# A seven-product matmul pass whose PSUM tiles go from two banks to one

## The chip, the cores and the metric

One NeuronCore of a Trainium2 chip runs the whole program. The metric is device time in microseconds, the median of three runs. A profile is one more execution, recorded by the hardware profiler.

## The reference

Attention over 4 batches, 12 heads, 448 positions and head size 64, with RMS-normed queries and keys; its output, 1792 tokens by 768 features, goes through two MLPs with 2048 hidden features:

```python
x = attention(q, k, v, g_q, g_k)              # (4*448, 768)
h = np.maximum(x @ moe_w_in, 0.0)             # first MLP
x = (h * h) @ moe_w_out
h = x @ moe2_w_in                             # second MLP
g = np.maximum(h, 0.0) + alpha * np.minimum(h, 0.0)
return g @ moe2_w_out
```

All of it is fp32. A product is taken in three matmuls of rounded parts ("hi" and "lo"): hi·lo, hi·hi, lo·hi. The lo part is the rest, x minus hi, so each operand costs a copy (hi) and a subtraction (lo).

## The kernel before

Features lie on the 128 partitions and the 448 tokens of one batch in the free dimension. Attention and the first MLP run first; they end near 814 us. From there to the end the second MLP runs as **seven-product passes**: batches are taken in pairs (0, 1), then (2, 3), and a 2 by 2 block product (two feature halves, two batches) is formed with seven products instead of eight, from sums of weight blocks and sums of activation blocks, the *forms*.

`quad` (L950) is one group of seven products. An **up** group makes hidden features from the three k-chunks of xs and xt (63 matmuls); a **down** group takes the hidden forms of two or three up groups (42 or 63 matmuls). `run_passes` (L1144) gives the order, the same for both batch pairs: u0 u1 u2, d0 (three groups, e = 0, 1, 2), u3 u4, d1 (three), u5 u6 u7, d2 (three). Panel d0 uses the forms of u0 and u1, d1 those of u2 to u4, d2 those of u5 to u7. That is 2 x 1008 = 2016 matmuls.

A group has four accumulators, called b, a, c and a scratch one, t. In the kernel before they lie in two PSUM tiles of two banks each, [128, 2, 512]: a and c are the halves of one tile, b and t the halves of the other (L952 and L953). `BANK` says where a product accumulates: A11, S2, S3 and A22 in b, A12 in a, S1 and S4 in c. An up group runs A11, A12, S2, S1, S3, S4, A22; a down group A11, S1, S2, S4, S3, A12, A22.

What happens after a product is in `event`. For an up group (L1001): `keep` copies an accumulator to an SBUF buffer q (ScalarE), before the next product accumulates onto it; `plus` adds or subtracts (VectorE, L995); `prelu` needs relu(-x) in a scratch accumulator and relu(x) (ScalarE, L1012 to L1018) and joins them (VectorE, L1020); `split` writes the hi copy of a form (ScalarE, L254) and its lo rest (VectorE or GpSimd, L262). For p5 the scratch of `prelu` is t, for p1 it is a, for u2 it is c. Two of the splits, `split((a, 0), 3, 2)` and `split((b, 0), 5, 2)`, take both halves of a tile, 896 columns, in one copy and one subtraction. Down groups add accumulators into the sums in SBUF (L1080).

The order on each engine is written out ahead of time by a list planner (`Tasks`, L53). Each step has an urgency, a duration (`act`, `dve`, `pool2`, L191 to L208) and what it reads and writes; the planner always issues the step that can start first. It keeps the halves of a PSUM tile apart, (a, 0) and (a, 1); the waits in the program come from the tile framework, which sees the tiles. A tile goes back to its pool when its last step is planned, and an up or down group takes all its tiles before its first product. Every engine works off its own queue in order.

`x_pair` (L1110) prepares the activation forms of the second batch pair: per k-chunk four loads of y from DRAM on the SyncE queue, seven hi copies, seven lo rests and four subtractions, through buffers of the pool q, of which there are nine at that time. It is called in `run_passes` while the last three down groups (d2) of the first pair are planned; each call's loads may not be planned before one given product of those groups (`begun`).

PSUM pool m (four tiles of two banks) also serves the end of the first MLP, whose tasks are planned before `ts.run(1)` (L1158).

Of the kernel before, what the change touches and what calls it, by code (L numbers as in the profile page):

```python
# [194 lines left out]
def dve(n):  # L195
    return 0.07 + 0.00104 * n
# [22 lines left out]
def attention_relu2_mlp_prelu_mlp(ctx: ExitStack, tc: tile.TileContext, qkt, qk_tm, v, gb, alpha, ident, sel,  # L219
# [10 lines left out]
    def pooled(pool, name, n, shape, dtype):  # L230
        ts.pool(name, [pool.tile(shape, dtype, name=f"{name}{i}") for i in range(n)])
# [592 lines left out]
    def without():  # L824
        with ExitStack() as es:
            q1 = es.enter_context(tc.tile_pool(name="q1", bufs=1))
            pp = es.enter_context(tc.tile_pool(name="pp2", bufs=1, space=PSUM))
# [121 lines left out]

            def quad(n, order, form, chunks, group, key, event):  # L950

                a, b = Buf(pool="m"), Buf(pool="m")  # L952
                place = {"a": (a, 0), "c": (a, 1), "b": (b, 0)}  # L953
                opened = set()
                turn[0] += 7
                t0 = turn[0]
# [3 lines left out]
                made = None if key in kept7 else sums(n, group, t0 - 24)  # L960

                def psum(x):
                    return x[0].ap[:, x[1], :S]

                for j, name in enumerate(order):
                    x, f = place[BANK[name]], FORM[name]
                    ts.phase = 1 if ahead and j < 3 else 2
                    if key is None:
                        w = unit(name, n, made, t0 + j - 17, None, None)
                    elif made:  # L970
                        k = Buf(dram.tile([128, 2, n], F32, name=f"k7_{key}_{j}"))
                        w = unit(name, n, made, t0 + j - 17, k, None)
                        kept7.setdefault(("made", key), []).append(k)
                    else:
                        w = unit(name, n, None, t0 + j - 17, None, kept7[key][j])
                    ts.phase = 2
                    start = BANK[name] not in opened
                    opened.add(BANK[name])
                    src = [form(f, k) for k in chunks]

                    for kk, get in enumerate(src):
                        def emit(e, w=w, x=x, kk=kk, get=get, fresh=start and not kk, more=not start, end=kk == len(src) - 1):
                            for part, h in ((0, 1), (0, 0), (1, 0)):
# [13 lines left out]
            def up(stage, q):  # L997
                s = slot_b[q % 3]
                p1, u2, p5 = (Buf(pool="q") for _ in range(3))

                def event(name, a, b, soon, psum):  # L1001
                    def ap(x):
                        return (lambda: x.ap) if isinstance(x, Buf) else (lambda: psum(x))
# [20 lines left out]
                    def split(x, f, n=1):  # L1024
                        def to(h):
                            return s.ap[:, f:f + n, h, :] if n > 1 else s.ap[:, f, h, :]

                        inside = isinstance(x, Buf)
                        items = [x] if inside else [(x[0], c) for c in range(2)]
                        src = ap(x) if inside else (lambda: x[0].ap[:, :, :S])  # L1030
                        add(soon, {"A": act(n * S, not inside)}, lambda e: copy(e, to(0), src()), items,
                            [(s, (f + i, 0)) for i in range(n)])
                        add(soon, {"V": dve(n * S), **({"P": pool2(S)} if inside else {})}, lambda e: rest(e, to(1), src(), to(0)),
                            items + [(s, (f + i, 0)) for i in range(n)], [(s, (f + i, 1)) for i in range(n)], free=not inside)

                    def plus(x, i0, i1, op=ALU.add):
                        add(soon, {"V": dve(S)}, tensor(ap(x), ap(i0), ap(i1), op), [y for y in (i0, i1) if y is not x], [x],
                            free=not all(isinstance(y, Buf) for y in (i0, i1)))

                    if name == "A11":  # L1040
                        keep(p1, (b, 0))
                    elif name == "A12":
                        plus(p1, (a, 0), p1)
                        prelu(p1, (a, 0), q)
                        split(p1, 0)
                    elif name == "S2":
                        keep(u2, (b, 0))
                    elif name == "S1":
                        keep(p5, (a, 1))
                    elif name == "S3":  # L1050
                        plus(p5, (b, 0), p5)
                        prelu(p5, (b, 1), q + KF // 2)
                        split(p5, 2)
                    elif name == "S4":
                        plus(u2, (a, 1), u2)
                        prelu(u2, (a, 1), q)
                        plus((a, 1), u2, p1, ALU.subtract)
                        plus((a, 0), p5, (a, 1), ALU.subtract)
                        split((a, 0), 3, 2)
                        plus((b, 1), (a, 0), p1, ALU.subtract)  # L1060
                    else:
                        c21, x = Buf(pool="q"), (b, 0)
                        prelu(c21, x, q + KF // 2, x)
                        split(c21, 1)
                        plus((b, 0), c21, (a, 0), ALU.subtract)
                        split((b, 0), 5, 2)

                quad(UP, UP_ORDER, lambda f, k: x_form(f, k), range(KD // 2), up32[q], f"u{q}", event)

            def down(p, e, batches):  # L1070
                held = {}

                def event(name, a, b, soon, psum):
                    first = p == 0

                    def keep(k, t, d, x):
                        held[k] = total[t][d] if first else Buf(pool="q")
                        add(soon, {"A": act(S, True)}, lambda e: copy(e, held[k].ap, psum(x)), [x], [held[k]])

                    def plus(k, t, d, x):  # L1080
                        y, z = held.get(k), total[t][d]
                        if k == "c21" and first:
                            keep(k, t, d, x)
                        else:
                            y = y or z
                            add(soon, {"V": dve(S)}, tensor(lambda: y.ap, lambda: psum(x), lambda: y.ap, ALU.add), [x], [y], free=True)
# [1 line left out]
                                add(soon, {"V": dve(S), "P": pool2(S)}, tensor(lambda: z.ap, lambda: z.ap, lambda: y.ap, ALU.add),  # L1088
                                    [y], [z])
                        if p == len(PANELS) - 1:  # L1090
                            add(soon, {"S": load(512 * S)}, dma(lambda: out[batches[t], d], lambda: z.ap), [z], [])

                    if name == "A11":
                        keep("p1", 0, e, (b, 0))
                    elif name == "S1":
                        keep("p5", 1, e + 3, (a, 1))
                    elif name == "S2":
                        keep("u2", 1, e, (b, 0))
                    elif name == "S4":
                        plus("u2", 1, e, (a, 1))  # L1100
                    elif name == "S3":
                        plus("p5", 1, e + 3, (b, 0))
                    elif name == "A12":
                        plus("p1", 0, e, (a, 0))
                    else:
                        plus("c21", 0, e + 3, (b, 0))

                quad(128 * len(PANELS[p]), DN_ORDER, lambda f, k: h_form(f, k), PANELS[p], dn32[e][p], None, event)

# [34 lines left out]
            def run_passes():  # L1144
                turn[0] = 40000
                for stage, batches in enumerate(((0, 1), (2, 3))):
                    for step in ("u0", "u1", "u2", "d0", "u3", "u4", "d1", "u5", "u6", "u7", "d2"):
# [18 lines left out]
                for d in range(KD):  # L1166
                    total[t][d].ap = sums_out[:, t, d, :]

            def more(name, n, shape, dt):
                for i in range(n):  # L1170
                    ts.free[name].append((ts.ends["T"], 200 + i, qb.tile(shape, dt, name=f"{name}_{i}")))
# [73 lines left out]
```

## Time and profile before

| | us |
|---|---|
| median of 3 runs | 1332.03 |
| lowest and highest run | 1327.61, 1338.84 |
| the profiled execution, own time | 1334.32 |
| its span | 1332.5 |
| mean granted TensorE clock in it | 0.968 |

PE is TensorE's matmuls, PEld its weight loads, DVE VectorE, ACT ScalarE, POOL GpSimd, SPq the SyncE queue that issues DMAs. In brackets behind an instruction stands the time in which its engine sat idle before it, and what ended that. PEclk is the granted TensorE clock as a share of full speed. Names m, q, ws, forms, xs, xt are tiles with their numbers left out: m is the PSUM pool, q and ws are both buffers of the SBUF pool q.

### The profile page before, as it was taken

Reading aid. Unit: us, or ns where it says so; the run is one execution under the profiler, and the core shown is the slowest. Engines: PE = TensorE matmul, PEld = TensorE weight load, DVE = VectorE, ACT = ScalarE, POOL = GpSimd, SP = SyncE. Lnnn points to the kernel's source line nnn. Section 1 sums busy time; section 2 is a strip of 40 time slices with the busy share of each in tenths; the row PEclk is TensorE's granted clock in tenths of the full one; section 3 lists DMA queues with packets and bytes.
Section 4 is the critical chain, followed back from the end, with each engine's and each line's share of the span. In section 5 each row is a group of like instructions: output and inputs, shape, how many; then the busy total and the mean of one; then the engine's idle time right before and its main releaser. Section 6 shows DMA issues by size and latency. Waiting matters only on the chain. (4 is left out here: it accounts for less than half of the span.)

```text
span 1332.5 us, 17324 instructions
## 1 busy us (share of the span) xinstructions
PE 1200.9 (90%) x5502; PEld 1023.2 (77%) x5502; DVE 901.7 (68%) x1596; ACT 792.3 (59%) x1561; POOL 526.2 (39%) x492
## 2 busy tenths in 40 slices
PE   4996998978999999999999999898888888979878
PEld 2554777767888888899999998687776767769767
DVE  6789999999887877137776504676657856554363
ACT  5787888886899788425552124555357435453452
POOL 3344356453555244200000067545566442135245
PEclk7998999999999999999999999898999899999999
DMA  5145758896546433579999956424154353422622
GB/s 179 52 152 201 240 179 278 276 320 247 187 151 199 157 132 106 185 253 333 325 322 340 323 193 224 162 110 167 48 206 166 123 203 116 148 82 78 195 71 83
DMA packets 95803, 250.32 MB, mean 188 GB/s; under 512 B 11296, under 2 KB 30880, under 8 KB 95712
## 3 DMA queue, kind: packets, MB, share of 16 engines
q1 hardware_dynamic: 95712, 249.22, 55.2%
q8 instruction: 43, 0.70, 0.2%
q14 instruction: 48, 0.39, 0.1%
HBM read 178.32 MB, written 70.78 MB: 187 GB/s over the span
## 5 line engine op out<-in xcount | busy, mean ns | idle before, releaser
L984 PE MATMUL m<-forms,whl 128*128 128x448 f32 x1008 | 219.2, 378 | 23.5 <-DVE forms L262 15.5
L984 PEld LDWEIGHTS m<-forms,whl 128*128 128x128 f32 x1008 | 195.4, 195 | 46.3 <-DVE forms L262 17.0
L984 PE MATMUL m<-xt,whl 128*128 128x448 f32 x432 | 111.0, 399 | 39.2 <-DVE q L995 13.9
L350 PE MATMUL bank<-xs,whl 128*128 128x448 f32 x576 | 138.0, 372 | 1.5 <-DMA whl<-w 1.5
L984 PEld LDWEIGHTS m<-xt,whl 128*128 128x128 f32 x432 | 84.4, 204 | 62.0 <-DVE q L1020 17.5
L350 PE MATMUL bank<-hg,whl 128*128 128x448 f32 x576 | 129.0, 367 | 2.0 <-DMA whl<-w 1.6
L984 PE MATMUL m<-xs,whl 128*128 128x448 f32 x576 | 124.7, 369 | 6.4 <-DVE xs L262 4.4
L984 PEld LDWEIGHTS m<-xs,whl 128*128 128x128 f32 x576 | 109.0, 190 | 17.2 <-DVE xs L262 4.7
L282 ACT ACTIVATE ws<-raw 128x384 f32<-128x384 f32 (+1 forms) x112 | 67.2, 600 | 92.2 <-DMA raw<-in_w 80.0
L350 PEld LDWEIGHTS bank<-xs,whl 128*128 128x128 f32 x576 | 108.6, 191 | 12.8 <-DMA whl<-w 1.9
L350 PE MATMUL m<-xs,whl 128*128 128x448 f32 x576 | 117.5, 366 | 0.7 <-ACT q L254 0.7
L350 PEld LDWEIGHTS bank<-hg,whl 128*128 128x128 f32 x576 | 108.1, 189 | 11.8 <-DMA whl<-w 2.0
L350 PE MATMUL m<-hg,whl 128*128 128x448 f32 x576 | 116.9, 365 | 0.0
L687 DVE TENSOR_REDUCE mc<-bank 112x1 f32<-112x448 f32 x192 | 111.3, 615 | 7.9 <-PE bank L683 6.5
L262 POOL TENSOR_TENSOR whl<-raw,whl 128x384 fp32r<-128x384 f32 (+1 forms) x87 | 87.2, 1006 | 74.2 <-ACT whl L254 64.9
L350 PEld LDWEIGHTS m<-xs,whl 128*128 128x128 f32 x576 | 107.9, 188 | 10.4 <-ACT q L254 1.1
L350 PEld LDWEIGHTS m<-hg,whl 128*128 128x128 f32 x576 | 108.2, 188 | 8.5
L262 POOL TENSOR_TENSOR whl<-ws,whl 128x384 fp32r<-128x384 f32 (+2 forms) x57 | 77.6, 1369 | 89.9 <-ACT whl L254 65.9
L708 PE MATMUL bank<-mv,st 128*128 128x448 f32 (+2 forms) x352 | 100.1, 390 | 7.7 <-DVE rhl L262 2.7
L262 POOL TENSOR_TENSOR xs<-q,xs 128x448 fp32r<-128x448 f32 x13 | 15.2, 1184 | 227.3 <-DMA q<-y 225.2
L286 DVE TENSOR_SCALAR ws<-ws 128x384 f32<-128x384 f32 (+1 forms) x112 | 46.2, 416 | 80.3 <-ACT ws L282 79.9
L254 ACT ACTIVATE whl<-raw 128x384 fp32r<-128x384 f32 (+1 forms) x120 | 59.5, 498 | 63.0 <-PE m L984 53.8
(166 smaller groups left out, 2353.0 us busy)
## 6 DMA issues: line engine op xcount, KB each, us to landing
raw<-in_w SPq DMA_DIRECT2D x64, 384.0 KB
raw<-in_w SPq DMA_DIRECT2D x48, 512.0 KB
whl<-w SPq DMA_DIRECT2D x64, 384.0 KB
whl<-w SPq DMA_DIRECT2D x48, 512.0 KB
k_u<-whl SPq DMA_DIRECT2D x56, 384.0 KB
whl<-k_u SPq DMA_DIRECT2D x56, 384.0 KB
w<-whl SPq DMA_DIRECT2D x32, 384.0 KB
w<-whl SPq DMA_DIRECT2D x24, 512.0 KB
```

What stands on the lines that cost most here:

```text
L254: nc.scalar.activation(out=o, in_=i, func=ACTF.Copy)
L262: (nc.gpsimd if e == "P" else nc.vector).tensor_tensor(out=o, in0=x, in1=hi, op=ALU.subtract)
L282: lambda e: nc.scalar.activation(out=f.ap[:, :n], in_=half(1).bitcast(F32), func=ACTF.Abs), [raw], [f], "f")
L286: lambda e: nc.vector.tensor_scalar(out=f.ap[:, :n], in0=f.ap[:, :n], scalar1=TINY, scalar2=None, op0=ALU.max),
L350: nc.tensor.matmul(out=acc.ap[:, t, :S], lhsT=w.ap[:, part * n + 128 * kk:part * n + 128 * kk + 128], rhs=src(h, k0 + kk, t)[1](), start=( ...
L687: lambda e, t=t, pm=pm: nc.vector.reduce_max(out=mc.ap[:, t:t + 1], in_=pm.ap[:CP, :S], axis=AX.X),
L708: nc.tensor.matmul(out=pa.ap[:keys, :S], lhsT=s.ap[:rows, k, c:c + keys], rhs=m.ap[:rows, k, :], start=(k == 0), stop=(k == 1))
L984: nc.tensor.matmul(out=psum(x), lhsT=w.ap[:, part * n + 128 * kk:part * n + 128 * kk + 128], rhs=get(h)[1](), start=fresh and h == 1, stop ...
```

## The change

1. Pool m now ends with the first MLP (`es_a`). After `ts.run(1)` a new PSUM pool n of eight one-bank tiles is opened in its place, and each group takes four of them, one per accumulator.
2. Every form is split by itself. In S4, form 4 (c) is split before form 3 (a), and form 6 (t) as soon as it is there; form 5 (b) is left for the end.
3. `x_pair` is called after all three d2 groups are planned. The loads of its first chunk are tied to a product 6 chunk-steps later than before (the third product of the first group instead of the first), those of the second 3 later, those of the third 15 earlier (the last product of the second group instead of the fifth of the third). The urgencies come to the same numbers.

```diff
-            pooled(pp, "m", 4, [128, 2, 512], F32)
-            for name in ("wf", "wsum"):
+            for name in ("wf", "wsum", "n"):
                 ts.pool(name, [])
             es_a = es.enter_context(ExitStack())
+            pooled(es_a.enter_context(tc.tile_pool(name="pp2", bufs=1, space=PSUM)), "m", 4, [128, 2, 512], F32)
...
-                a, b = Buf(pool="m"), Buf(pool="m")
-                place = {"a": (a, 0), "c": (a, 1), "b": (b, 0)}
+                place = {c: Buf(pool="n") for c in "bact"}
...
-                    return x[0].ap[:, x[1], :S]
+                    return x.ap[:, :S]
...
-                                         [x] + ([(a, "slot"), (b, "slot")] if not j and not kk else []), "mlp"))
-                    event(name, a, b, soon, psum)
+                                         [x] + ([(y, "slot") for c, y in place.items() if c != BANK[name]] if not j and not kk else []), "mlp"))
+                    event(name, *place.values(), soon, psum)
...
+                    def split(x, f):
+                        inside = x not in banks
+                        add(soon, {"A": act(S, not inside)}, lambda e: copy(e, s.ap[:, f, 0, :], ap(x)()), [x], [(s, (f, 0))])
+                        add(soon, {"V": dve(S), **({"P": pool2(S)} if inside else {})},
+                            lambda e: rest(e, s.ap[:, f, 1, :], ap(x)(), s.ap[:, f, 0, :]), [x, (s, (f, 0))], [(s, (f, 1))],
+                            free=not inside)
...
                     elif name == "S4":
-                        plus(u2, (a, 1), u2)
-                        prelu(u2, (a, 1), q)
-                        plus((a, 1), u2, p1, ALU.subtract)
-                        plus((a, 0), p5, (a, 1), ALU.subtract)
-                        split((a, 0), 3, 2)
-                        plus((b, 1), (a, 0), p1, ALU.subtract)
+                        plus(u2, c, u2)
+                        prelu(u2, c, q)
+                        plus(c, u2, p1, ALU.subtract)
+                        plus(a, p5, c, ALU.subtract)
+                        split(c, 4)
+                        split(a, 3)
+                        plus(t, a, p1, ALU.subtract)
+                        split(t, 6)
                     else:
...
-                        plus((b, 0), c21, (a, 0), ALU.subtract)
-                        split((b, 0), 5, 2)
+                        plus(b, c21, a, ALU.subtract)
+                        split(b, 5)
...
                             down(i, e, batches)
-                            if not stage and step == "d2":
-                                x_pair((2, 3), e, turn[0] - 8, begun[-(21, 21, 9)[e]])
+                        if not stage and step == "d2":
+                            for k, n in enumerate((-57, -39, -24)):
+                                x_pair((2, 3), k, turn[0] - 22 + 7 * k, begun[n])
...
+            pp = es.enter_context(tc.tile_pool(name="pp3", bufs=1, space=PSUM))
...
+            more("n", 8, [128, 512], F32, pp)
```

The other steps name b, a, c, t in place of the halves, and are else as before.

## Rows read from the trace of the kernel before

**Rows 1.** The page: busy time, share of the span, instructions, of each engine.
```profile
PE 1200.9 (90%) x5502; PEld 1023.2 (77%) x5502; DVE 901.7 (68%) x1596; ACT 792.3 (59%) x1561; POOL 526.2 (39%) x492
```

**Rows 2.** Busy time by stretch: all seven-product passes; undisturbed downs; a slow stretch.
```profile
core 0: us, PE busy (x) PEld busy (x) DVE busy (x) ACT busy (x) POOL busy (x), PEclk, DMA share, GB/s
814.30:1328.60 514.30, 445.13 (x2017) 388.61 (x2015) 310.03 (x488) 253.64 (x490) 239.73 (x216) 0.95 0.39 136
950.60:976.60 26.00, 26.00 (x128) 23.61 (x127) 14.53 (x24) 9.13 (x18) 17.23 (x15) 1.00 0.30 107
1055.80:1059.20 3.40, 3.40 (x9) 3.03 (x10) 2.51 (x3) 1.35 (x4) 1.45 (x1) 0.50 0.16 59
```

**Rows 3.** Busy time by stretch: the six runs of up groups, and their sum.
```profile
814.30:868.90 54.60, 45.06 (x190) 38.25 (x189) 35.04 (x53) 32.59 (x65) 29.25 (x29) 0.91 0.53 194
...
1236.00:1283.70 47.70, 40.69 (x190) 34.86 (x189) 22.01 (x34) 25.33 (x47) 11.35 (x12) 1.00 0.48 146
sum 272.50, PE 226.88 PEld 193.35 DVE 151.42 ACT 154.17 POOL 110.66; mean PE 37.81 PEld 32.22 DVE 25.24 ACT 25.69 POOL 18.44
```

**Rows 4.** What PE waited for, 814 to 1333 us: total, times, longest.
```profile
PE m L984 <- DVE forms L262: 15.5, 4, 4.2
PE m L984 <- DVE q L995: 14.3, 10, 2.3
PE m L984 <- DVE q L1020: 12.2, 14, 1.2
PE m L984 <- ACT m L1014: 6.8, 11, 0.7
PE m L984 <- DVE ws L1020: 6.3, 7, 1.2
PE m L984 <- ACT q L254: 5.3, 1, 5.3
```

**Rows 5.** Timeline of the up groups u1 and u2 of the second pair.
```profile
1112.33 0.68 DVE L1020 SCALAR_TENSOR_TENSOR q<-m,minus_alpha,q 128x448 f32<-128x448 f32 x1 [0.66 <-ACT m L1014]
...
1113.07 0.88 PE L984 MATMUL m<-xt,whl 128*128 128x448 f32 x3 [0.84 <-DVE q L1020]
...
1120.54 0.87 PE L984 MATMUL m<-xt,whl 128*128 128x448 f32 x3 [1.12 <-DVE q L995]
```

**Rows 6.** Busy time by stretch: the four first groups of d1 and d2, summed.
```profile
sum 74.90, PE 59.44 PEld 52.81 DVE 52.08 ACT 34.23 POOL 41.77; mean PE 14.86 PEld 13.20 DVE 13.02 ACT 8.56 POOL 10.44
```

**Rows 7.** Timeline from S4 of u4 to the first down group, second pair.
```profile
1194.50 0.92 ACT L254 ACTIVATE forms<-m 128x896 fp32r<-128x896 f32 x1
1195.45 0.63 DVE L995 TENSOR_TENSOR m<-m,q 128x448 f32<-128x448 f32 x1 [0.98 <-ACT forms L254]
...
1196.65 1.08 DVE L262 TENSOR_TENSOR forms<-m,forms 128x896 fp32r<-128x896 f32 x1
...
1197.79 1.49 PE L984 MATMUL m<-forms,whl 128*128 128x448 f32 x3 [4.17 <-DVE forms L262]
```

**Rows 8.** Groups by line and shape: count, busy us, mean ns, idle before.
```profile
L254 ACT ACTIVATE forms<-m 128x896 fp32r<-128x896 f32 x32 | 29.4, 917 | 16.9 <-DVE m L995 16.8
L254 ACT ACTIVATE q<-m 128x448 f32<-128x448 f32 x63 | 33.9, 545 | 71.7 <-PE m L984 52.5 <-PE m L350 11.5 <-DVE q L1020 5.2
L262 DVE TENSOR_TENSOR forms<-m,forms 128x896 fp32r<-128x896 f32 x32 | 34.5, 1081 | 0.0
L262 DVE TENSOR_TENSOR hl<-bank,hl 128x448 fp32r<-128x448 f32 x90 | 55.1, 618 | 26.6 <-ACT bank L716 25.0 <-PE pv L751 0.8
```

**Rows 9.** The change of batch pair: a stretch of d2, then u0, timelines.
```profile
1042.90:1062.90 20.00, 14.67 (x65) 13.12 (x64) 17.05 (x25) 8.95 (x19) 8.97 (x7) 0.83 0.39 127
...
1076.40:1097.60 21.20, 15.05 (x64) 12.68 (x63) 8.37 (x11) 9.01 (x18) 8.44 (x9) 0.92 0.67 237
...
1076.05 0.58 ACT L254 ACTIVATE xs<-q 128x448 fp32r<-128x448 f32 x1 [6.95 <-DMA q<-y]
...
1087.06 1.49 PE L984 MATMUL m<-xs,whl 128*128 128x448 f32 x3 [4.36 <-DVE xs L262]
```

More of the change, by code (lines that the diff above doesn't have):

```diff
@@ L826, in without @@
             q1 = es.enter_context(tc.tile_pool(name="q1", bufs=1))
-            pp = es.enter_context(tc.tile_pool(name="pp2", bufs=1, space=PSUM))
             xt = [fixed(q1, [128, 2, KD // 2, S], F32R, f"xt{i}") for i in range(3)]
             pooled(q1, "q", 4, [128, S], F32)
-            pooled(pp, "m", 4, [128, 2, 512], F32)
-            for name in ("wf", "wsum"):
+            for name in ("wf", "wsum", "n"):
                 ts.pool(name, [])
             es_a = es.enter_context(ExitStack())
+            pooled(es_a.enter_context(tc.tile_pool(name="pp2", bufs=1, space=PSUM)), "m", 4, [128, 2, 512], F32)
             hg = fixed(es_a.enter_context(tc.tile_pool(name="qa", bufs=1)), [128, 2, KF, 2, S], F32R, "hg2")
@@ L999, in up, with event @@
                 p1, u2, p5 = (Buf(pool="q") for _ in range(3))
-                def event(name, a, b, soon, psum):
+                def event(name, b, a, c, t, soon, psum):
+                    banks = (b, a, c, t)
                     def ap(x):
-                        return (lambda: x.ap) if isinstance(x, Buf) else (lambda: psum(x))
+                        return (lambda: psum(x)) if x in banks else (lambda: x.ap)
                     def keep(to, x):
@@ L1022, in prelu @@
                             [tmp, al_b], [x], free=True)
[L1024 to L1034, printed above, removed]
+                    def split(x, f):
[4 more added lines that the diff above has]
+                            free=not inside)
@@ L1036, in plus @@
                     def plus(x, i0, i1, op=ALU.add):
                         add(soon, {"V": dve(S)}, tensor(ap(x), ap(i0), ap(i1), op), [y for y in (i0, i1) if y is not x], [x],
-                            free=not all(isinstance(y, Buf) for y in (i0, i1)))
+                            free=i0 in banks or i1 in banks)
                     if name == "A11":
-                        keep(p1, (b, 0))
+                        keep(p1, b)
                     elif name == "A12":
-                        plus(p1, (a, 0), p1)
@@ L1044, in event @@
-                        prelu(p1, (a, 0), q)
+                        plus(p1, a, p1)
+                        prelu(p1, a, q)
                         split(p1, 0)
                     elif name == "S2":
-                        keep(u2, (b, 0))
+                        keep(u2, b)
                     elif name == "S1":
-                        keep(p5, (a, 1))
+                        keep(p5, c)
                     elif name == "S3":
-                        plus(p5, (b, 0), p5)
-                        prelu(p5, (b, 1), q + KF // 2)
+                        plus(p5, b, p5)
@@ L1053, in event @@
+                        prelu(p5, t, q + KF // 2)
                         split(p5, 2)
                     elif name == "S4":
-                        plus(u2, (a, 1), u2)
-                        prelu(u2, (a, 1), q)
-                        plus((a, 1), u2, p1, ALU.subtract)
-                        plus((a, 0), p5, (a, 1), ALU.subtract)
-                        split((a, 0), 3, 2)
-                        plus((b, 1), (a, 0), p1, ALU.subtract)
-                    else:
-                        c21, x = Buf(pool="q"), (b, 0)
-                        prelu(c21, x, q + KF // 2, x)
+                        plus(u2, c, u2)
@@ L1064, in event @@
+                        prelu(u2, c, q)
[5 more added lines that the diff above has]
+                        split(t, 6)
+                    else:
+                        c21 = Buf(pool="q")
+                        prelu(c21, b, q + KF // 2, b)
                         split(c21, 1)
-                        plus((b, 0), c21, (a, 0), ALU.subtract)
@@ L1071, in down, with event, keep, plus @@
                 held = {}
-                def event(name, a, b, soon, psum):
+                def event(name, b, a, c, t, soon, psum):
                     first = p == 0
-                    def keep(k, t, d, x):
-                        held[k] = total[t][d] if first else Buf(pool="q")
+                    def keep(k, i, d, x):
+                        held[k] = total[i][d] if first else Buf(pool="q")
                         add(soon, {"A": act(S, True)}, lambda e: copy(e, held[k].ap, psum(x)), [x], [held[k]])
-                    def plus(k, t, d, x):
-                        y, z = held.get(k), total[t][d]
+                    def plus(k, i, d, x):
+                        y, z = held.get(k), total[i][d]
                         if k == "c21" and first:
-                            keep(k, t, d, x)
+                            keep(k, i, d, x)
                         else:
@@ L1090, in plus @@
                         if p == len(PANELS) - 1:
-                            add(soon, {"S": load(512 * S)}, dma(lambda: out[batches[t], d], lambda: z.ap), [z], [])
+                            add(soon, {"S": load(512 * S)}, dma(lambda: out[batches[i], d], lambda: z.ap), [z], [])
                     if name == "A11":
-                        keep("p1", 0, e, (b, 0))
+                        keep("p1", 0, e, b)
                     elif name == "S1":
-                        keep("p5", 1, e + 3, (a, 1))
+                        keep("p5", 1, e + 3, c)
                     elif name == "S2":
-                        keep("u2", 1, e, (b, 0))
+                        keep("u2", 1, e, b)
                     elif name == "S4":
-                        plus("u2", 1, e, (a, 1))
+                        plus("u2", 1, e, c)
                     elif name == "S3":
-                        plus("p5", 1, e + 3, (b, 0))
+                        plus("p5", 1, e + 3, b)
                     elif name == "A12":
-                        plus("p1", 0, e, (a, 0))
+                        plus("p1", 0, e, a)
                     else:
-                        plus("c21", 0, e + 3, (b, 0))
+                        plus("c21", 0, e + 3, b)
                 quad(128 * len(PANELS[p]), DN_ORDER, lambda f, k: h_form(f, k), PANELS[p], dn32[e][p], None, event)
@@ L1167, in without, with more @@
                     total[t][d].ap = sums_out[:, t, d, :]
-            def more(name, n, shape, dt):
+            pp = es.enter_context(tc.tile_pool(name="pp3", bufs=1, space=PSUM))
+            def more(name, n, shape, dt, pool=qb):
                 for i in range(n):
-                    ts.free[name].append((ts.ends["T"], 200 + i, qb.tile(shape, dt, name=f"{name}_{i}")))
+                    ts.free[name].append((ts.ends["T"], 200 + i, pool.tile(shape, dt, name=f"{name}_{i}")))
             more("wf", 1, [128, 4 * UP], F32)
```

## The prediction

> **What bounds the kernel now.** The page comes first: TensorE is busy for 90% of the span, the vector engine for 68%, the others less [rows 1]. So TensorE sets the time, and the question is where it stands still. Busy time by stretch answers it. The seven-product passes take 514.3 us for 2016 matmuls [rows 2]. What they would take undisturbed is read from two down groups with full PE time and a granted clock of 1.00: 26.0 us for 126 matmuls, 0.206 us each, 13.0 us for a group of 63 [rows 2]. 2016 at that rate are 416 us, so 98 us of this stage are lost, and the change touches this stage alone. By group: the sixteen up groups take 272.5 us [rows 3] instead of 16 x 13.0 = 208; the four down groups that follow directly on an up group whose forms they need (first group of d1 and d2) take 74.9 [rows 6] instead of 52.0; the second d2 group of the first batch pair takes 20.0 instead of 13.0, and u0 of the second pair 21.2 instead of 13.0 [rows 9]. The rest of the downs is near its floor.
>
> Next the waits: PE's largest are for forms (L262), for `plus` (L995), and three entries for `prelu` (L1020 twice, L1014) [rows 4]. The entries of `prelu` are the key. L1020 reads a scratch accumulator and writes an SBUF buffer that no matmul reads; L1014 writes a scratch accumulator. No product needs either. Yet the timeline shows the last chunk of A22 start only when L1020 has ended, after 0.84 us idle, and the first chunk of S1, which writes c, wait 1.12 us for the `plus` that reads a [rows 5]. In both cases the accumulator that the matmul writes and the one that the other engine touches are halves of one two-bank tile. So the waits are of the tile, not of the bank. L1020, L1014 and nine of the ten waits for q L995 (S1 after A12; the tenth is a down group's A12 after S4, on the same tile) are of this kind: 14.3 + 12.2 + 6.8 + 6.3 = 39.6 us of idle [rows 4]. A wait costs more than its idle entry, as the next matmul must be filled in again, and after long ones TensorE runs at half clock: in the stretch at 1055.8 the granted clock is 0.50, which is 1.2 GHz, and nine matmuls take 3.40 us instead of 1.86 [rows 2].
>
> **The change part by part.**
>
> *One tile per accumulator.* The false waits go. What they cost is taken from the stretches: 272.5 - 208 = 64.5 us over the ups, less what has another cause: of the 8.2 us in u0 of the second pair some 6.9 (4.36 us idle for xs forms [rows 9], a smaller one, and the half clock after them; the rest are its own two false waits). 57 us are left. What is late next: the true waits. S2, S3 and S4 must wait until `keep` has copied b, b and c, and A22 until `plus` has read b; each has one other product (9 x 0.206 = 1.9 us) between, against 0.55 us for a copy and 0.62 for a subtraction [rows 8] and the handover. That fits where the queues of ScalarE and VectorE are not behind. In the ups of the second pair VectorE is busy for 22.0 of 47.7 us [rows 3], and I leave 0.45 us per group. In the first pair the weights are still summed and split, and VectorE is busy for 35.0 of 54.6 us [rows 3]; three undisturbed groups would take 39 us, so it would be at 90%, and its in-order queue will hold up a `plus` or, through ScalarE's, a `keep`. I leave 1.2 us per group there. Together 8 x 0.45 + 8 x 1.2 = 13, gain 44. Bounds: everything goes (57), or the first pair keeps 2 us per group and the second 0.9, together 23 (34).
>
> *Forms split singly.* In the first group of d1 and d2, S1 on the last chunk needs form 4, the difference c, of the up group just ended. Today its copy waits for a too, takes 0.92 us at 1194.50 with form 3 in the same instruction, and its lo rest starts behind two more subtractions at 1196.65 and takes 1.08; TensorE stands for 4.17 us [rows 7]. After the change the copy can follow c itself, one subtraction earlier, and copy and rest are shorter by 0.37 and 0.46 us [rows 8]; the rest no longer queues behind the subtractions for t and b (0.63 us each [rows 7]) and the 0.98 us that t waits for the double copy. That is 2.5 to 4 us sooner. TensorE, without A22's false wait, wants it 1.0 us sooner too. I leave 2 us of standing and 0.8 us of half clock in each of four groups: of 74.9 - 52 = 22.9 us, 11 stay, gain 12. Bounds: 5 (the queue order stays, only the instructions are shorter) and 19 (the wait falls under 1 us and the clock stays up).
>
> *What the split costs.* Per up group two copies of 917 ns become four of 545, two subtractions of 1081 ns four of 618 [rows 8] (the last of them is the nearest row of a 448-column rest out of PSUM): +0.35 us on ScalarE, +0.31 on VectorE, over 16 groups 5.5 and 5.0 us. Beside TensorE they cost nothing while those queues have room; in the first pair's ups VectorE has little, so I charge half of VectorE's, 2.5 us (bounds 0 and 5). The Trainium skill (Perfetto Trace Analysis, Optimizing Scalar/DVE Operations) speaks against the step: each instruction pays a fixed access time, about 125 ns on DVE and 51 ns on ScalarE out of PSUM, and grouping pays where the engine is saturated. By its figures the 32 extra instructions would cost, as an estimate, 4.0 and 1.6 us instead of the 5.0 and 5.5 of the rows; the trace agrees in kind, and neither is near the gain.
>
> *`x_pair` moved.* Twelve loads on SyncE's queue, 21 copies, 21 rests and 12 subtractions change place, none is added. The third chunk's loads, for which ScalarE stood 6.95 us at 1076.05 and TensorE 4.36 us in u0 [rows 9], may go 15 chunk-steps (15 x 3 x 0.206 = 9 us) earlier; they then pass on SyncE's queue the stores of d2's sums and the weight loads of u0. That should remove most of u0's 6.9 us. The first two chunks go 3.7 and 1.9 us later. Against it: each call takes four of nine q buffers and each down group three, so two calls and a group want eleven; a `keep` that gets none holds TensorE, as in the 20.0 us group, where PE waited 5.3 us for ACT q L254 [rows 4, 9]. Such a wait may move rather than go. Of 7.0 + 6.9 us I take a gain of 6; bounds -7 (one more such hold with its half clock) and +14.
>
> *Small ones.* A down group's A12 waits for the `plus` on c through the tile as well, some 1.5 us in all (0 to 2.5). The new PSUM pool lies over the old one: if u0's first product must wait for the last copies of the first MLP, that is at most two of 0.55 us [rows 8] and the handover, 1.3 us; I take 0.3, as the first bank is probably one long out of use.
>
> Sum: 44 + 12 + 6 + 1.5 - 2.5 - 0.3 = 61 us. The profiled execution took 1334.3 us, 2.3 above the median of the runs; 1334.3 - 61 = 1273, on the median's footing **1271 us**. The bounds added up: gains of 57 + 19 + 14 + 2.5 = 92 (1240) and 34 + 5 - 7 + 0 - 5 - 1.3 = 26 (1306).
>
> **The rivals.**
>
> *The stall comes back as a true wait.* TensorE runs into VectorE's and ScalarE's queues in the first pair. For it: 90% of VectorE there. Against it: POOL can take rests, and the downs leave VectorE a third of its time. In the first run of ups 5.2 us are lost per group today ((54.6 - 39) / 3). If the first pair's eight groups keep 3.2 of that, the first downs gain only half, `x_pair` nothing and the split costs its full 5 us, the gain is 57 - 8 x 3.2 - 3.6 + 6 + 0 - 5 = 29 us: 1303.
>
> *The waits do not go.* If the waits came from the order in which one engine counts its steps, and not from the tile, one-bank tiles would leave them. For it: a semaphore counts all of an engine's instructions. Against it: the released matmul starts right behind the one instruction on its own tile, group after group. Then only the splits and `x_pair` pay: 12 x 2/3 + 6 - 2.8 = 11 us, 1321, within 1%.
>
> *The clock falls.* The long waits of today become many short ones, in every product, and TensorE drops to 1.2 GHz not for a few matmuls but for whole groups. Place: the ups of the first pair. Price: 3.40 / 9 - 0.206 = 0.172 us per matmul [rows 2], 10.8 us per group of 63. It decides from six groups on (6 x 10.8 = 65 us, more than the gain); at all eight the kernel would take 1271 + 87 = 1358. Against it: with waits of up to 1.2 us the granted clock is 1.00 in the last run of ups [rows 3], and it fell after long ones. The Trainium skill knows such a case (TensorE: Matmul & The Clock Gate, A second HAM failure mode: psum-queue depth-cycling): cycling through PSUM banks with small idles made the clock swing between its levels. That rule would give the 1358; the trace of before does not bear it out.
>
> **How the numbers follow.** Forecast with its bounds 0.77, true waits 0.14, waits stay 0.04, clock 0.03, anything else 0.02. The first and second rivals lie at 1303 and 1321, so the range goes from 1244 to 1306. 1% is 13 us, about what a measurement of this kernel can tell from no change: faster than 1319 in the first two cases and some of the rest, 0.92; within 1%, 0.05; slower, 0.03.
>
> **What would show it.** Right: no PE wait for L1020 or L1014 in the passes; the second pair's ups at 13.0 to 13.5 us each; forms L262 waits of about 2 us in d1 and d2; no wait for xs in u0. Wrong: PE waits for q L254 or q L995 before S2, S3, S4, A22 in the first pair (true waits); L1020 still there (waits stay); a granted clock near 0.5 over whole ups (clock); a PE wait for ACT q in d2 longer than 5 us (buffers of q).

## The result, and the profile after

The changed kernel takes **1261.61 us** (median of four runs, 1260.60 to 1262.90); the kernel before, in the same session, took 1331.80. The ratio is 0.9468 with a 95% interval of 0.9427 to 0.9510. That is 70 us less, where 61 were forecast. The profiled execution took 1261.38 us with a span of 1259.6, 72.9 below the span before.

In the changed kernel's lines, matmuls of the passes are L982, `plus` is L993, and the copies, rests and `prelu` keep their numbers; its PSUM tiles are named n. The page's busy row answers to [rows 1]:

```profile
PE 1177.3 (93%) x5502; PEld 1016.9 (81%) x5502; DVE 908.8 (72%) x1632; ACT 794.5 (63%) x1596; POOL 527.3 (42%) x485
```

Busy time by stretch follows, with the columns of [rows 2]: all seven-product passes, then the two undisturbed downs.

```profile
815.30:1255.80 440.50, 418.83 (x2016) 380.58 (x2016) 318.11 (x523) 254.25 (x523) 236.17 (x208) 0.98 0.47 159
923.90:949.50 25.60, 25.60 (x128) 23.71 (x128) 16.22 (x27) 8.72 (x17) 18.48 (x15) 1.00 0.30 109
```

The stage went from 514.3 to 440.5 us, 73.8 less: all of the gain. At the rate of its own undisturbed downs (25.6 us for 126 matmuls) 2016 take 410 us, so 31 us are still lost where 98 were.

The six runs of up groups, the first and the fifth row and their sum, against 272.50 us in [rows 3]; then the sum over the first groups of d1 and d2, against 74.90 in [rows 6]:

```profile
815.30:856.30 41.00, 39.30 (x189) 35.21 (x190) 33.52 (x54) 31.22 (x68) 26.53 (x25) 1.00 0.73 259
...
1105.90:1136.10 30.20, 27.40 (x128) 24.93 (x127) 12.63 (x21) 15.70 (x32) 7.80 (x8) 0.94 0.54 176
...
sum 212.10, PE 207.60 PEld 190.04 DVE 145.04 ACT 144.50 POOL 103.37; mean PE 34.60 PEld 31.67 DVE 24.17 ACT 24.08 POOL 17.23
```

```profile
sum 62.30, PE 54.83 PEld 47.90 DVE 59.02 ACT 38.29 POOL 45.40; mean PE 13.71 PEld 11.98 DVE 14.75 ACT 9.57 POOL 11.35
```

All that PE waited for from 814 to 1262 us, where [rows 4] showed six entries of 5 us and more:

```profile
PE n L982 <- ACT ws L254: 8.4, 2, 7.2
PE n L982 <- DVE forms L262: 6.3, 4, 2.8
PE n L982 <- DMA whl<-k_u: 2.8, 1, 2.8
PE n L982 <- DVE q L993: 1.8, 2, 1.2
PE n L982 <- ACT sums_out L254: 1.6, 2, 1.4
PE n L982 <- DVE sums_out L993: 0.8, 1, 0.8
PE n L982 <- ACT q L254: 0.5, 1, 0.5
PE n L982 <- DVE ws L993: 0.5, 1, 0.5
```

No entry for L1020 or L1014 is left. The shorter of the two ACT ws waits, 1.2 us, is A11 of the very first up group, which waits for the last copies of the first MLP out of pool m, as the new pool n lies in its place; it ends at 815.25 us, just ahead of the stretch above.

PE's timeline through u1 of the second pair shows what took the place of the false waits. In [rows 5] there were idle times of 0.84 and 1.12 us in brackets; here no row has a bracket:

```profile
1053.18 5.63 PE L982 MATMUL n<-xs,whl 128*128 128x448 f32 x27
1058.66 3.81 PE L982 MATMUL n<-xt,whl 128*128 128x448 f32 x18
1062.30 1.99 PE L982 MATMUL n<-xs,whl 128*128 128x448 f32 x9
1064.13 1.99 PE L982 MATMUL n<-xt,whl 128*128 128x448 f32 x9
```

The wait for forms is shorter but there, as the timeline of the second pair's first d1 group shows; it answers to [rows 7]:

```profile
1138.70 0.55 ACT L254 ACTIVATE forms<-n 128x448 fp32r<-128x448 f32 x1
1139.28 0.63 DVE L993 TENSOR_TENSOR n<-ws,n 128x448 f32<-128x448 f32 x1
...
1139.82 0.62 DVE L262 TENSOR_TENSOR forms<-n,forms 128x448 fp32r<-128x448 f32 x1
...
1140.49 1.29 PE L982 MATMUL n<-forms,whl 128*128 128x448 f32 x5 [1.16 <-DVE forms L262]
```

The copy of c is a single one, the rest starts 0.57 us after it, behind one subtraction (that for a) and not two, and PE stands for 1.16 us instead of 4.17.

The largest wait left is S4's in the second d2 group of the first pair, where `keep` had no free buffer q until a sum had been read out of one (columns as in [rows 9]):

```profile
1018.17 0.54 ACT L254 ACTIVATE ws<-n 128x448 f32<-128x448 f32 x1 [2.16 <-DVE ws L993]
...
1018.76 1.49 PE L982 MATMUL n<-forms,whl 128*128 128x448 f32 x3 [7.18 <-ACT ws L254]
```

### The profile page after: what moved, and what is told of

It is laid out like the page before. It is cut to its first block, busy times and chain, and to the rows that moved or that the text cites. A ratio compares the mean times of both kernels' runs of the same rounds, so it can differ in the third digit from the quotient of the medians.

```text
span 1259.6 us, 17375 instructions
## 1 busy us (share of the span) xinstructions
PE 1177.3 (93%) x5502; PEld 1016.9 (81%) x5502; DVE 908.8 (72%) x1632; ACT 794.5 (63%) x1596; POOL 527.3 (42%) x485
## 4 chain that ended last, share of the span: by engine, by line
PE 63%; DVE 17%; ACT 9%; DMA 6%; issue 4%; SPq 1%; POOL 0%; ACTq 0%; DVEq 0%; POOLq 0%
PE n L982 26%; PE m L350 14%; PE bank L350 10%; PE bank L708 4%; PE pv L751 4%; PE pv L727 3%; DMA raw<-in_w 3%; DVE mc L687 2%; PE bank L683 2%; DVE ws L293 2%; DVE ws L296 2%; DVE n L993 1%; DMA whl<-w 1%; DVE ws L286 1%; DMA tm<-in_qk_tm 1%
## 5 line engine op out<-in xcount | busy, mean ns | idle before, releaser
L982 PE MATMUL n<-forms,whl 128*128 128x448 f32 x1008 | 212.1, 371 | 17.2 <-ACT ws L254 7.2
L982 PEld LDWEIGHTS n<-forms,whl 128*128 128x128 f32 x1008 | 190.7, 190 | 37.6 <-DVE forms L262 8.2
L982 PE MATMUL n<-xs,whl 128*128 128x448 f32 x576 | 124.2, 369 | 4.0 <-DMA whl<-k_u 2.8
L982 PEld LDWEIGHTS n<-xs,whl 128*128 128x128 f32 x576 | 109.1, 190 | 14.1 <-DMA whl<-k_u 3.2
L350 PE MATMUL m<-xs,whl 128*128 128x448 f32 x576 | 118.0, 366 | 1.6 <-DMA whl<-w 0.9
L350 PEld LDWEIGHTS m<-xs,whl 128*128 128x128 f32 x576 | 107.9, 188 | 11.7 <-ACT q L254 1.1
L262 POOL TENSOR_TENSOR whl<-ws,whl 128x384 fp32r<-128x384 f32 (+2 forms) x57 | 80.5, 1422 | 83.3 <-ACT whl L254 61.1
L262 POOL TENSOR_TENSOR whl<-raw,whl 128x384 fp32r<-128x384 f32 (+1 forms) x87 | 89.9, 1037 | 50.8 <-ACT whl L254 42.8
L262 POOL TENSOR_TENSOR xs<-q,xs 128x448 fp32r<-128x448 f32 x11 | 13.3, 1213 | 229.1 <-DMA q<-y 226.8
L982 PE MATMUL n<-xt,whl 128*128 128x448 f32 x432 | 93.7, 366 | 1.7 <-DVE q L993 1.2
L262 DVE TENSOR_TENSOR hl<-bank,hl 128x448 fp32r<-128x448 f32 (+1 forms) x120 | 73.8, 619 | 27.8 <-ACT bank L716 25.4
```

Source lines behind the costliest of these rows:

```text
L262: (nc.gpsimd if e == "P" else nc.vector).tensor_tensor(out=o, in0=x, in1=hi, op=ALU.subtract)
L350: nc.tensor.matmul(out=acc.ap[:, t, :S], lhsT=w.ap[:, part * n + 128 * kk:part * n + 128 * kk + 128], rhs=src(h, k0 + kk, t)[1](), start=( ...
```

## The experiments

Theory: a wait on a PSUM tile holds whatever touches either of its banks, and one tile per accumulator removes it; the splits shorten the first downs; `x_pair` moves a shortage of q buffers about. Rivals: the gain is that of the written order (single splits, another order of the planner's), or of `x_pair`.

### Tiles alone

The changed kernel, with two accumulators as halves of one tile, each half a buffer of its own to the planner:

```diff
...
-            more("n", 8, [128, 512], F32, pp)
+            for i in range(2):
+                two = pp.tile([128, 2, 512], F32, name=f"nbt_{i}")
+                ts.free["nb"].append((ts.ends["T"], 200 + i, two[:, 0, :]))
+                ts.free["nt"].append((ts.ends["T"], 200 + i, two[:, 1, :]))
...
```

Both pairs (b with t, a with c):

> The changed kernel, but its eight accumulators lie again as halves of four two-bank tiles (b with t, a with c); splits and the moved loads stay. Theory (the waits are of the tile): TensorE waits for L1018-type prelu steps (scratch accumulators) and for plus in S1 and A22 come back, some 57 us: 1312 to 1325 us. Rival (the gain came from the single splits and the moved loads, the waits follow the count of steps): 1258 to 1270 us, no such waits.

Only a with c, and only b with t:

> Only a and c share a two-bank tile, b and t have one each. Theory: S1 (which writes c) waits again for the steps that read or write a: in the trace of before these gaps are 29.7 us and some 8.7 of half clock behind them, and A12 of the downs about 1.5: 1290 to 1306 us; A22 does not wait for prelu. Rival: 1258 to 1270 us.

> Only b and t share a two-bank tile. Theory: A22 (which writes b) waits again for the prelu in t: in the trace of before 17.9 us and 2.1 of half clock: 1275 to 1288 us; S1 does not wait for a's steps. Rival: 1258 to 1270 us.

Both pairs, and all four buffers held to the group's last product, as in the kernel before:

```diff
-[x] + ([(y, "slot") for c, y in place.items() if c != BANK[name]] if not j and not kk else [])
+[x] + ([(y, "slot") for c, y in place.items() if c != BANK[name]] if not j and not kk or j == 6 and kk == len(src) - 1 else [])
```

> As the run with both pairs in two-bank tiles, but a group holds its four accumulators to its last product, so that b always lies with t of its own group and a with its own c, as in the kernel before. Theory: the waits of S2 for forms steps (t of the group before lay with b) go, those of S1 and A22 stay: 1316 to 1332 us. Rival (the pairing does not matter, the single splits themselves cost time in two-bank tiles): 1335 to 1343 us.

| | time, us | ratio to before (95%) | sixteen ups, us |
|---|---|---|---|
| changed kernel | 1261.61 | 0.9468 (0.9427 to 0.9510) | 212.1 |
| a, c paired | 1291.46 | 0.9683 (0.9639 to 0.9727) | 241.4 |
| b, t paired | 1293.59 | 0.9707 (0.9657 to 0.9756) | 238.5 |
| both paired | 1339.30 | 1.0042 (1.0016 to 1.0068) | 270.0 |
| both, held as before | 1326.77 | 0.9937 (0.9916 to 0.9958) | 270.6 |

In all four kernels the instructions stand in the order of the changed kernel on TensorE, VectorE, ScalarE and GpSimd from 816 us to the end; only the tiles differ, and the time with both paired is 1339.3 instead of 1261.6. So the tile is the cause, and the written order is not. The ups nearly add up: 29.3 us for a and c, 26.4 for b and t, 57.9 for both. The whole times do not: 29.9 and 32.0 us, but 77.7 for both, where the downs are longer too. The largest of PE's waits on the paired tiles after 814 us, in the kernels with one pair each, name the halves:

```profile
PE nac L982 <- DVE q L993: 10.5, 6, 2.4
PE nac L982 <- DVE q L1020: 7.5, 10, 0.8
```

```profile
PE nbt L982 <- DVE nbt L993: 5.7, 5, 1.2
...
PE nbt L982 <- ACT forms L254: 5.1, 8, 0.9
PE nbt L982 <- DVE q L1020: 3.4, 4, 0.9
```

Where a and c share, S1 and S4 (onto c) wait for the `plus` and the L1020 that read a. Where b and t share, A22 waits for L1020, as in [rows 5]; and S2 waits for work on the group before (the first entries of the second fence). That wait was not in the expectation, and it is why b with t came out above its range: the planner frees t early, and as buffers of their own b and t of one tile go to different groups. Both paired has this too, and came out above its range (1312 to 1325) as well. Held to the end, S2 has no such wait. In the ups that changes nothing (270.0 and 270.6 us: where S2 waits no longer, A22 waits again); the gain is in the downs, 71.2 against 66.1 us in the four first downs. The kernel with the pairs held is the kernel before but for single splits and `x_pair`: 1326.8, 0.6% below before.

### What the moved `x_pair` is worth

In the changed kernel, its old place:

```diff
-                        if not stage and step == "d2":
-                            for k, n in enumerate((-57, -39, -24)):
-                                x_pair((2, 3), k, turn[0] - 22 + 7 * k, begun[n])
+                            if not stage and step == "d2":
+                                x_pair((2, 3), e, turn[0] - 8, begun[-(21, 21, 9)[e]])
```

> The changed kernel with the loads of the second pair's forms called where they were before. Theory: the wait for xs forms in u0 of the second pair comes back (7 us with its half clock) and the wait for a q buffer in d2 falls by 2: 1264 to 1270 us. Rival (the place of the loads does not matter, the wait only changes its place): 1259 to 1263 us.

In the kernel before, the reverse edit, the new place and nothing else:

> The kernel before with the moved loads of the second pair's forms alone. Theory (the third chunk's loads were late): u0 of the second pair loses its waits for xs, some 7 us, d2 keeps a wait for a q buffer: 1323 to 1329 us. Rival (the wait only changes its place): 1330 to 1335 us.

The old place in the changed kernel gave 1264.65 us (ratio 0.9504, 0.9439 to 0.9568), which overlaps with the changed kernel; the new place in the kernel before 1333.64 (ratio 1.0001, 0.9974 to 1.0027), no difference. Busy time by stretch shows it: the second and third d2 group of the first pair, u0 of the second, and their sum. First the changed kernel with the old place, then the kernel before with the new one:

```profile
1008.30:1029.90 21.60, 14.76 (x64) 13.21 (x63) 18.80 (x29) 9.90 (x21) 9.06 (x7) 0.84 0.35 110
1029.90:1043.40 13.50, 13.05 (x65) 11.77 (x64) 7.48 (x10) 3.56 (x7) 12.88 (x12) 1.00 0.56 173
1043.40:1061.60 18.20, 14.66 (x64) 12.87 (x63) 8.16 (x11) 8.26 (x16) 7.46 (x7) 0.91 0.75 261
```

```profile
1043.20:1065.50 22.30, 14.77 (x65) 12.86 (x64) 19.70 (x29) 10.20 (x21) 10.37 (x8) 0.85 0.39 127
1065.50:1084.10 18.60, 14.73 (x64) 12.88 (x63) 17.95 (x21) 6.27 (x13) 12.56 (x10) 0.91 0.56 167
1084.10:1099.10 15.00, 13.31 (x65) 11.68 (x64) 3.87 (x6) 5.75 (x11) 1.92 (x3) 1.00 0.75 254
```

In the kernel before these three took 20.0, 13.5 and 21.2 us; the new place there takes 6.2 from u0 and gives 7.4 to the d2 groups. In the changed kernel they take 21.7, 12.8 and 12.8 with the new place against the 21.6, 13.5 and 18.2 above: 6.0 less here, of which the first d2 group gives back 1.7 (17.8 against 16.1 with the old place).

Two kernels went at the wait that is left. One lets the loads have five of the nine buffers only, so that four are left to the groups' copies:

```diff
...
-                    b, src = Buf(pool="q"), y_dram[bt][k + 3 * half]
+                    b, src = Buf(pool=("q", "qx") if batches[0] == 0 else "qx"), y_dram[bt][k + 3 * half]
...
```

> The changed kernel, but five of the nine q buffers alone may take the second pair's loads, so that four are left for the copies of the groups. Theory (the loads hold all nine, and a copy without a buffer holds TensorE): the 7.2 us wait of PE for ACT ws L254 before S4 in the second d2 group is gone; the loads wait instead, and u0 waits for xs forms: 1254 to 1268 us. Rival (ScalarE's queue was late for another reason): the wait before S4 stays at 7 us: 1260 to 1264 us.

1264.01 us (ratio 0.9485, 0.9446 to 0.9524): no gain. The same d2 group, then u0 of the second pair:

```profile
1005.40:1018.20 12.80, 12.80 (x65) 11.87 (x64) 12.15 (x18) 6.38 (x13) 9.43 (x7) 1.00 0.45 150
...
1031.00:1058.20 27.20, 18.30 (x64) 15.18 (x63) 8.63 (x11) 11.20 (x21) 17.69 (x16) 0.69 0.57 184
```

S4's wait is gone, and u0 is 14.4 us longer, waiting for xs.

The other has ten buffers, and a 768 KB weight load out of the way of u3's weights, an edit that was first tried alone:

```diff
...
-                made = None if key in kept7 else sums(n, group, t0 - 24)
+                made = None if key in kept7 else sums(n, group, t0 - 24, begun[-30] if late else None)
...
-            more("whl", 2, [128, 2 * S], F32R)
-            more("q", 2, [128, S], F32)
+            more("whl", 2, [128, 2 * UP], F32R)
+            more("q", 3, [128, S], F32)
```

> The changed kernel, but in the second pair the 768 KB load of the weights of d1's first group may not be planned before u3's A22 region, about 30 chunk-steps ahead of its use, instead of just before u3's own weight loads. Theory (that load delays the weights of u3's A12, for which TensorE waits 2.8 us and then runs at 1.2 GHz): the wait is gone, 1256 to 1259 us. Rival (the weight load is late because its buffer comes free late): the wait stays, 1260 to 1263 us.

> The changed kernel with one more buffer q in this stage (ten instead of nine; paid for by two buffers of the weight pool that are 768 instead of 896 columns long) and with the 768 KB load for the second pair's second d1 panel later, so that u3's weights pass first on SyncE's queue. Theory (the waits left over are a shortage of one buffer and a load in the way): the 7.2 us wait of S4 in the second d2 group of the first pair falls below 2 us, the 2.8 us wait of A12 in u3 goes, with the half clock behind both 8 to 14 us less than the changed kernel, 1248 to 1254. Rival (x_pair as a whole comes too late for the time that the three d2 groups take, so a buffer only moves the wait to another product): PE's waits between 988 and 1060 us stay at 8 to 12 us in sum, and the time is 0 to 5 us below the changed kernel, 1256 to 1262.

> The changed kernel once more, as the yardstick of the three runs beside it: 1258 to 1265 us by every theory.

The load alone gave 1258.86 us (ratio 0.9443, 0.9406 to 0.9480), both together 1261.31 (0.9451, 0.9421 to 0.9482), the changed kernel beside the latter 1263.94 (0.9471, 0.9441 to 0.9501): none of them can be told from another. PE's wait for DMA in u3 is not listed in either, but in this second profile of the changed kernel it was 0.4 us, not 2.8: the u3 stretch varies by itself. With ten buffers S4's wait becomes one of S3, 6.2 us long:

```profile
PE n L982 <- ACT q L254: 7.1, 2, 6.2
```

So one buffer more is not enough. Whether any number would be, and whether the forms of the second pair can be made any sooner at all, was not tried.

### How much room VectorE has

The prediction held VectorE to be at 90% in the first pair's ups and charged that twice. Here it takes lo rests of an up group a second time, writing the same numbers again, two of them or four:

```diff
+                        if f in (3, 5):
+                            add(soon, {"V": dve(S)}, lambda e: rest(e, s.ap[:, f, 1, :], ap(x)(), s.ap[:, f, 0, :]),
+                                [x, (s, (f, 0))], [(s, (f, 1))], free=True)
```

> The changed kernel in which VectorE takes two of the lo rests of every up group (forms 3 and 5) twice: the second writes the same numbers once more, 32 instructions of 0.62 us, 1.24 us per up group, four times what the change itself added to VectorE. In the first pair's up groups VectorE goes from about 81% to 91% of the stretch. Theory (VectorE's queue has room, and a true wait has one product of slack): 0 to 3 us more than the changed kernel, 1261 to 1265. Rival (the prediction's: at 90% its in-order queue holds TensorE by some 1.2 us in each of the first pair's eight up groups, which PE's waits for q L993 or q L254 there would show): 8 to 12 us more, 1269 to 1274.

> As the run before it, with all four lo rests after S4 and A22 (forms 3, 4, 5 and 6) taken twice: 2.5 us per up group on VectorE, which takes it to about 100% in the first pair's up groups and 80% in the second's. Theory (room until the queue is full): the first pair's ups are now held, 1 to 2 us in each of eight, and the first group of d1 and d2 waits 0.6 us longer for form 4: 10 to 20 us more than the changed kernel, 1271 to 1282. Rival (VectorE is not what sets the ups at all): at most 4 us more, from the four first downs alone, 1262 to 1266.

Two gave 1275.55 us (ratio 0.9563, 0.9529 to 0.9597), four 1294.55 (0.9702, 0.9673 to 0.9731), against 1263.94: 11.6 and 30.6 us more. Both lie above the theory's range; two rests come out just above the rival's 1269 to 1274. But the place is the rival's only in part. The sums of busy time over the first pair's eight ups: the changed kernel's second profile, two, four:

```profile
sum 105.70, PE 104.19 PEld 94.14 DVE 85.04 ACT 81.27 POOL 72.32; mean PE 34.73 PEld 31.38 DVE 28.35 ACT 27.09 POOL 24.11
```

```profile
sum 110.20, PE 105.51 PEld 93.98 DVE 89.68 ACT 80.23 POOL 69.23; mean PE 35.17 PEld 31.33 DVE 29.89 ACT 26.74 POOL 23.08
```

```profile
sum 117.10, PE 109.46 PEld 97.35 DVE 97.57 ACT 78.06 POOL 71.44; mean PE 36.49 PEld 32.45 DVE 32.52 ACT 26.02 POOL 23.82
```

The ups lose 4.5 and 11.4 us, 0.6 and 1.4 per group, where the rival has 1.2 for two rests. The four first downs, 61.4 us in the changed kernel's second profile, take 68.1 and 75.9. With two rests VectorE's busy time in these ups grows by 4.6 us where 9.9 were added (8 x 2 x 0.62), so it doesn't reach the expected 91%: half of the work is handed on to the downs behind. TensorE's waits for forms hardly grow, 7.4 us in all against 6.2; the first d2 group of the first pair, 3.5 us longer, waits for weights (whl) and `plus` too. The second rest also makes its own form ready 0.6 us later, so not all of this is VectorE's load; the two are not separated.

With four, the waits for forms are 13.0 us, up to 3.7 each, and `plus` into the sums holds the first d0 group of the two pairs for 3.8 and 2.9 us. The ups' loss is then nearly all in u2 and u7 of the first pair, where S4 waits for weights that VectorE copies; in u2:

```profile
856.53 1.79 PE L982 MATMUL n<-xs,whl 128*128 128x448 f32 x3 [2.69 <-DVE whl L258]
```

## Why the prediction was right, and where its sizes were off

**What bounds the kernel: right.** TensorE set the time, the loss lay in the passes, and the waits were of the tile; the paired kernels show it.

**The ups: right in kind, gain under-sized.** Without u0's 6.9 us, which stood under `x_pair`, the ups gained 60.4 - 6.9 = 53.5 us against 44, inside the bounds of 34 to 57; some 3 of them, as an estimate, are the pace of the last section. Of the 13 us left to true waits the first pair was to keep 9.6. It keeps 105.3 - 8 x 12.8 = 2.9, most of it in u0 and u1. The step that failed is "it would be at 90%": it divided VectorE's 35.0 us by 39 us, but in the changed kernel VectorE is busy for 33.5 of the first run's 41.0 us, 82%, and S2, S3, S4 and A22 have one product to wait in. Part of VectorE's work has moved out of the ups: by the sums above it is busy there for 145.0 us instead of 151.4, and in the four first downs for 59.0 instead of 52.1. With more load TensorE is held, as the doubled rests show, and more in the first downs than in the ups, a place that the step did not have. The second pair's ups took 12.8 each but for u3 (promised: 13.0 to 13.5). The term did not have u3's 17.5 us, in which PE waited 2.8 us for weights and the granted clock was 0.94 over the run; it is not stable, 13.5 us in the second profile.

**The first downs: right in sum, with some luck.** 74.9 - 62.3 = 12.6 us gained, 12 forecast; waits for forms L262 of 6.3 us in four, 1.6 each (2 were left). But three of the four gained 3.8 to 4.6 us, more than forecast, and the first d2 group of the first pair nothing: it took 17.6 us and takes 17.8, with a forms wait of 2.8 us. With `x_pair` in its old place it takes 16.1. The Trainium skill (Perfetto Trace Analysis, Optimizing Scalar/DVE Operations) has, beside the rule on grouping, one for this: where Scalar and Vector aren't saturated but cause bubbles on other engines, breaking up instructions may let work end sooner. The trace agrees, 4.17 to 1.16 us in the timelines. The order in which the splits are written has no part in it: with the old order, the planner gives the same program. How much of the 12.6 belongs to single splits, and how much to tiles, the kernel with both pairs held as before shows, as it has single splits in two-bank tiles. The sum over its four first downs, and its waits for forms before S1 (1.0 us more stand before S2):

```profile
sum 66.10, PE 56.80 PEld 47.28 DVE 58.60 ACT 34.66 POOL 39.85; mean PE 14.20 PEld 11.82 DVE 14.65 ACT 8.67 POOL 9.96
```

```profile
PE nac L982 <- DVE forms L262: 5.9, 4, 2.1
```

So 74.9 - 66.1 = 8.8 us come with the splits, close to the two thirds of 12 that the second rival left them, and 3.8 with the tiles. The whole kernel is then 0.6% faster than before.

**What the split costs: not seen by itself.** On the page VectorE is busy for 7.1 us more than before and ScalarE for 2.2, where the working had 5.0 and 5.5. By mean lengths the change added 0.31 us per up to VectorE, two doubled rests 1.24 us, and those cost 11.6 us. A quarter of that, as an estimate, is 2.9 us; 2.5 were charged. It is rather too much: twice the rests cost 30.6 us, so the cost grows faster than the load. The part on ScalarE was not tried.

**`x_pair`: a gain of 6 taken, some 4 found.** Promised and seen: u0 waits for no xs. Also seen is what was feared, "such a wait may move rather than go": S4 in d2 waits for 7.2 us where the sign for wrong was 5. By the stretches above the new place is worth 6.0 - 1.7 = 4.3 us in the changed kernel and nothing in the kernel before; by the times alone it can't be told from nothing.

**The small terms.** The new PSUM pool cost more than the 0.3 us taken: "probably one long out of use" was wrong, and A11 of the first up group waits for 1.17 us, near the bound of 1.3. It stands ahead of the passes, which is why these gained 73.8 us and the span 72.9.

**Rivals.** "The stall comes back as a true wait" did not happen at this load of VectorE (1303 forecast); with two doubled rests it comes in part, with A22 waiting 0.3 to 0.8 us for `plus` in five of the first pair's ups. "The waits do not go" is refuted. "The clock falls": the granted clock is 1.00 in five of the six runs of ups. The Trainium skill's rule on cycling through PSUM banks with small idles (TensorE: Matmul & The Clock Gate, A second HAM failure mode: psum-queue depth-cycling) does not show here: eight single banks are cycled through, and the idles went away with the tiles.

**The sum by stretches:** ups 60.4, first downs 12.6, second d2 group 20.0 - 21.7 = -1.7, and 2.5 for the other downs, most of it pace, 73.8 in all.

## What to carry to other kernels

Look at what a waiting matmul writes and at what its releaser touches: if they are two halves of one tile, the wait is false, and a tile per bank removes it. Price what is handed on to the next stage too: an engine with 80% load may hardly hold TensorE where the load is, and hold it in the stage behind. A wait for buffers that moves when the loads are moved shows its price only when the stretches on both sides are summed.

## What had not been expected of the hardware

TensorE's matmuls run at two paces, 2% apart, at a granted clock that the rows give as 1.00. In the second profile of the changed kernel, u3 and u4 of the first pair and u1 and u2 of the second have the same 126 matmuls and no wait to speak of:

```profile
888.60:914.60 26.00, 26.00 (x128) 23.62 (x127) 20.20 (x32) 19.17 (x39) 17.12 (x17) 1.00 0.69 255
...
1058.10:1083.60 25.50, 25.50 (x128) 23.63 (x127) 18.88 (x33) 18.30 (x39) 8.25 (x8) 1.00 0.58 167
```

The kernel before had 26.0 in [rows 2], the changed kernel 25.6 in its first profile. Over 208 us of ups that is 3 us. As both paces stand in one execution, it is not the change's; why it is so stays open.
